# Layer 2 of an attention and two-MLP kernel, in blocks of 512 tokens

## The chip, the core and the metric

The kernel runs on one core of a Trainium2 chip. TensorE (PE) multiplies matrices: it loads a weight tile and streams columns past it into a bank of PSUM. VectorE (DVE), ScalarE (ACT) and GpSimd (POOL) do elementwise work, SyncE (SP) issues the DMAs. The metric is device time of one execution in microseconds (us), the median of several runs. The granted clock is the share of TensorE's full speed of 2.4 GHz that the chip allows; its other level is 1.2 GHz.

## The reference

Three stages, one after the other. The first is a linear-attention recurrence over 768 steps, for 4 batches and 8 heads of width 40. Its output, 3072 tokens of 320 values, goes through two layers of one form:

```python
x = attn_out.transpose(0, 2, 1, 3).reshape(3072, 320)
h = np.maximum(x @ w_in, 0.0)      # layer 1: w_in 320 x 2048
x = h * h @ w_out                  # w_out 2048 x 320
h = x @ w_in2                      # layer 2, weights of its own
r = np.maximum(h, 0.0)
out = (r * r) @ w_out2
```

## The kernel before

**Recording and planning.** The kernel does not issue its instructions as it meets them. Each call is recorded as a task with the cells of memory that it reads and writes. `_Plan.run` (L320) then plays the tasks through a model of the five engines: it has a cost for each form, and for each engine a heap of ready tasks ordered by `plan.prio`, lowest first. Whichever engine is free earliest takes its best ready task. The order that comes out is fixed; on the chip each engine runs its own list in that order and waits for semaphores. `plan.either` (L181) records a task that can go to one of several engines; for DVE the planner asks whether another engine would be done within 800 model ns of it, and if so leaves the task there. All recorded instructions have the line L69, so tiles and shapes tell them apart.

**Split numbers.** Every product is made of numbers split in a high and a low part (`xh`, `xl` and so on), and of the four partial products three are computed, so a matrix product is three matmuls.

**The two layers.** 3072 tokens are 12 blocks of 256 (`NBLK`). The hidden width of 2048 is 16 slices f of 128 (`NF`). `in_step` (L899) makes one slice: eight matmuls of 256 columns, weights `wi` stationary, tokens moving, into one bank (`HB`, banks 4 and 5). `gate` (L1001) makes relu, square, the high part `m_h` and the low part `m_l` of the slice, three of them in flight (`NG`). Relu and square are ACT's; the cast to `m_h` may go to ACT or DVE, the subtraction for `m_l` to DVE or POOL. `out_step2` (L938) of layer 2 then makes, for both halves of 128 tokens, three matmuls of 320 columns with the gate stationary and `wo` moving; two banks gather the 16 slices. Even and odd blocks use banks 0, 1 and 2, 3. `block2` (L1095) runs this for a block, copies the two banks to `m_o`, one on ACT and one on DVE, and sends them out in four DMAs. Layer 1 (`block1`, L1008) has its output transposed: 16 matmuls of 256 columns per slice, gathered in banks 6 and 7, and a zeroing matmul of 512 columns at the start of each block.

**The order of stages.** Attention, the decoding of layer 1's weights and layer 1 are planned together until the attention is over (L1078). Then layer 2's weights get their room and are decoded (`decode_w2`, 36 pieces of a DMA and some ten elementwise instructions on ACT, DVE and POOL); what is left of layer 1 and all of layer 2 is recorded and run. Gates have priorities from -200 up, inputs -100 (`P_X`), decoding 2.7 (`P_D`), matmuls from 1000 up (L1023). So PE does the earliest block first and takes a later slice when an earlier gate is not ready. `load_x` (L948) puts a block's input in the one staging tile `m_x`; `split_x` (L953) splits it into `m_xh` and `m_xl`, two buffers for even and odd blocks, used by both layers. `check_w` (L1126) tests the decays' range with 16 reductions on DVE.

Of the kernel before, what the change touches and what calls it, by code (L numbers as in the profile page):

```python
# [26 lines left out]
NF = 16  # L27
# [45 lines left out]
class _Plan:  # L73
# [5 lines left out]
    def __init__(self, nc):  # L79
        self.V = _Engine(self, nc.vector, "DVE")  # L80
        self.A = _Engine(self, nc.scalar, "ACT")
        self.G = _Engine(self, nc.gpsimd, "POOL")
        self.T = _Engine(self, nc.tensor, "PE")
        self.D = _Engine(self, nc.sync, "SP")
        self.tasks = []
        self.wr, self.rd = {}, {}
        self.cache = {}
        self.prio = 0.0
        self.tag = None
        self.open = None  # L90
        self.left = {}
        self.done = {}
        self.free = dict.fromkeys(self.LAT, 0.0)
        self.avail = {e: [] for e in self.LAT}
        self.pend = {e: [] for e in self.LAT}
        self.succ = {}
        self.npred = {}
        self.ready = {}
        self.mode = None
        self.first = None  # L100
        self.ticks = {}
        self.dma = 0.0
        self.held = {}

    def group(self):
        return _Group(self)
# [71 lines left out]
        else:  # L178
            self.add([rec])

    def either(self, *calls):  # L181

        alts, first = {}, None
        for f in calls:
            self.open = []
            f()
            recs, self.open = self.open, None
            first = first or recs
            alts[recs[0][0]] = ([r[1] for r in recs], sum(r[2] for r in recs), max(r[5] for r in recs))
        self.add(first, alts)  # L190

    def add(self, ops, alts=None):
        if not ops:
            return
        i = len(self.tasks)
# [31 lines left out]
        alts = alts or {eng: ([o[1] for o in ops], cost, max(o[5] for o in ops))}  # L227
        self.tasks.append((alts, self.prio, nbytes, self.tag, k))
        self.left[self.tag] = self.left.get(self.tag, 0) + 1
        live = [q for q in preds if q not in self.done]  # L230
        self.npred[i] = len(live)
        self.ready[i] = dict.fromkeys(alts, 0.0)
# [3 lines left out]
            else:  # L236
                self.succ.setdefault(q, []).append(i)
        if not live:
            for e in alts:
                heapq.heappush(self.pend[e], (self.ready[i][e], i))  # L240

    def after(self, q, i):
        t, e = self.done[q]
# [76 lines left out]
    def run(self, until=None):  # L320
        while until is None or self.left.get(until, 0):
# [57 lines left out]
            for j in self.succ.pop(i, ()):  # L379
                self.after(i, j)  # L380
                self.npred[j] -= 1
                if not self.npred[j]:
                    for z in self.tasks[j][0]:
                        heapq.heappush(self.pend[z], (self.ready[j][z], j))


@with_exitstack
def rwkv7_two_mlp_kernel(
# [60 lines left out]
    dx = [mm[:, 2304:3264], mm[:, 3264:4224]]  # L449
    nid0 = moe.tile([128, 192], F32R, name="nid")  # L450
    nid = nid0[:, 64:192]
    m_xh = [moe.tile([128, 3, 256], F32R, name=f"m_xh{i}") for i in range(2)]
    m_xl = [moe.tile([128, 3, 256], F32R, name=f"m_xl{i}") for i in range(2)]
    m_h = [moe.tile([128, 256], F32R, name=f"m_h{i}") for i in range(NG)]
    m_l = [moe.tile([128, 256], F32R, name=f"m_l{i}") for i in range(NG)]
    m_x = pad[:, 0:768].rearrange("p (k t) -> p k t", k=3)
# [305 lines left out]
    def copy(engs, o, i):  # L762
        calls = []
        for eng in engs:
            calls.append((lambda: A.copy(out=o, in_=i)) if eng is A else (lambda eng=eng: eng.tensor_copy(out=o, in_=i)))
        plan.either(*calls)
# [14 lines left out]
    def add(eng, o, x, y):  # L781
        tt2(eng, o, x, y, ALU.add)
# [155 lines left out]
    def out_step2(w, f, i, ob):  # L938
        gh = m_h[i % NG]
        gl = m_l[i % NG]  # L940
        for s in range(2):
            o = slice(s * 128, s * 128 + 128)
            with plan.group():
                T.matmul(ob[s][:, 0:320], gh[:, o], w[2][:, f, 0:320], start=(f == 0), stop=False)
                T.matmul(ob[s][:, 0:320], gh[:, o], w[2][:, f, 320:640], start=False, stop=False)
                T.matmul(ob[s][:, 0:320], gl[:, o], w[2][:, f, 0:320], start=False, stop=(f == NF - 1))

    def load_x(src_a, src_b):  # L948
        D.dma_start(out=m_x[:, 0:2], in_=src_a)
        for s in range(2):  # L950
            D.dma_start(out=m_x[64 * s:64 * s + 64, 2], in_=src_b)

    def split_x(xh, xl):  # L953
        copy(AV, xh, m_x)
        sub(VG, xl, m_x, xh.bitcast(F32))
# [43 lines left out]
        V.memset(bank[i], 0.0)  # L999

    def gate(h, i):  # L1001
        gg, gh, gl = m_r[i % 2], m_h[i % NG], m_l[i % NG]
        A.activation(out=gg, in_=h, func=AF.Relu)
        A.activation(out=gg, in_=gg, func=AF.Square)
        copy(AV, gh, gg)
        sub(VG, gl, gg, gh.bitcast(F32))

# [74 lines left out]
    def make_w2():  # L1082
        pool = w2x.enter_context(tc.tile_pool(name="w2", bufs=1))
        w = alloc_w(pool, 2)
        d = [pool.tile([128, 960], F32, name=f"dt{i}") for i in range(2)]
        plan.prio = P_D
        decode_w2(w, win2, win32, wout2, dx + d)
        return w, d, pool
# [6 lines left out]
    def block2(m, at, rows):  # L1095
# [14 lines left out]
        for s in range(2):  # L1110
# [3 lines left out]
            for h in range(2):  # L1114
                D.dma_start(out=rows(s, h), in_=o[64 * h:64 * h + 64])

    orow = out.rearrange("(p s u t) d -> p s u t d", p=NP, s=2, u=NU)
    wflat = nat[3].rearrange("b t d -> (b t d)").rearrange("(p x) -> p x", p=128)
    WC = wflat.shape[1]
# [20 lines left out]
        V.tensor_reduce(out=wrow[:, 256:257], in_=wrow[:, 0:256], axis=AX.X, op=ALU.max)  # L1140
        V.tensor_copy(out=wbad, in_=wrow[:, 256:257])

    for m in range(NBLK):
        block2(m, m, lambda p, s: orow[p, s, m])
        if m == min(3, NBLK - 1):
            check_w()
    plan.run()
    sched.__exit__(None, None, None)
# [45 lines left out]
    with tc.If(bad > 0):  # L1194
        with tc.tile_pool(name="gen", bufs=1) as gen:
            general_attention(gen)
        w2 = make_w2()[0]
        plan.run()
        with tc.For_i(0, NU) as q:
            block1(0, q)  # L1200
            block2(0, q, lambda p, s: orow[p, s, bass.ds(q, 1)].rearrange("o t d -> (o t) d"))
            plan.run()
        w2x.close()
# [78 lines left out]
```

## Time and profile before

| | us |
|---|---|
| median of 3 runs | 1207.71 (1205.3 to 1211.73) |
| profiled execution | 1209.43 |
| its span, first to last instruction | 1207.6 |
| PE busy | 1104.0 (91%) |
| DVE, ACT, POOL busy | 805.9, 747.5, 388.2 |
| mean granted clock | 0.955 |

A busy time is an average over stages. Until about 716 us the attention and layer 1 share the engines; then layer 1 and the decoding of layer 2's weights; from about 876 us layer 2 is alone. An instruction of the profile stands as output tile <- input tiles; PE's duration of one matmul is longer than the distance between two, since they overlap, so the distance of starts is what counts.

### The profile page before, as it was taken

The numbers are of one execution on the slowest core, as the hardware profiler recorded it, in microseconds if no ns is written. First come the engines' busy times: TensorE is split into PE (matmuls) and PEld (weight loads), VectorE is DVE, ScalarE is ACT, GpSimd is POOL, SyncE is SP. The second block draws the span as 40 slices with busy tenths as digits, with TensorE's granted clock in tenths as the row PEclk, the third lists the DMA queues.
The fourth block names the chain that finished last, engine by engine and source line by source line (L and its number), as shares of the span: only waits on it lengthen the run. The fifth ranks groups of instructions, "written<-read, shape, count | busy, mean of one in ns | idle before, by whom it ended". The sixth has DMA issues, their size and how long they took to land.

```text
span 1207.6 us, 43193 instructions
## 1 busy us (share of the span) xinstructions
PE 1104.0 (91%) x18096; PEld 1032.2 (85%) x18096; DVE 805.9 (67%) x1786; ACT 747.5 (62%) x2077; POOL 388.2 (32%) x443
## 2 busy tenths in 40 slices
PE   3888898998989998899899999999899999999996
PEld 2656787887878887798789899999899999999996
DVE  6887888789888978999798746666773232222221
ACT  4496554555565565556446468888666666666664
POOL 7544334223323332343224117776820000000000
PEclk9986789999998999999899999999899999999999
DMA  8555343155325515533451322332241010101000
GB/s 244 143 154 146 85 104 103 57 127 146 79 70 138 136 49 127 143 90 78 123 121 36 60 74 84 93 93 82 79 140 36 25 29 24 33 24 27 13 12 14
DMA packets 142239, 103.86 MB, mean 86 GB/s; under 512 B 98001, under 2 KB 110162, under 8 KB 142034
## 3 DMA queue, kind: packets, MB, share of 16 engines
q1 hardware_dynamic: 142034, 101.00, 31.5%
q8 instruction: 144, 2.36, 0.8%
q14 instruction: 61, 0.50, 0.1%
HBM read 82.88 MB, written 11.80 MB: 78 GB/s over the span
## 4 chain that ended last, share of the span: by engine, by line
PE 50%; DVE 7%; ACT 3%; issue 2%; DMA 1%; POOL 1%; SPq 1%; DVEq 0%; ACTq 0%; POOLq 0%
PE bank L69 50%; DVE mm L69 3%; DVE q L69 2%; ACT mm L69 1%; ACT q L69 1%; SPq L69 1%; DVE x L69 0%; DVE y L69 0%; DVE kt L69 0%; ACT m_h L69 0%; DMA v<-in_el_dram 0%; POOL kb L69 0%; DMA lk<-kt 0%; DVE p L69 0%; DMA mm<-in_win_dram 0%
## 5 line engine op out<-in xcount | busy, mean ns | idle before, releaser
L69 PE MATMUL bank<-m_xh,wi 128*128 128x256 f32 x1920 | 387.0, 286 | 9.7 <-ACT mm L69 5.4
L69 POOL TENSOR_TENSOR m_l<-mm,m_h 128x256 fp32r<-128x256 f32 x200 | 162.8, 816 | 546.3 <-ACT m_h L69 293.7
L69 PEld LDWEIGHTS bank<-m_xh,wi 128*128 128x128 f32 x1920 | 315.3, 193 | 13.2 <-ACT mm L69 6.0
L69 PE MATMUL bank<-m_xl,wi 128*128 128x256 f32 x1152 | 324.2, 285 | 1.8 <-POOL m_xl L69 1.8
L69 ACT ACTIVATE mm<-bank 128x256 f32<-128x256 f32 x384 | 146.2, 382 | 233.1 <-PE bank L69 214.3
L69 DVE TENSOR_TENSOR m_l<-mm,m_h 128x256 fp32r<-128x256 f32 x184 | 85.0, 462 | 217.6 <-ACT m_h L69 209.7
L69 PEld LDWEIGHTS bank<-m_xl,wi 128*128 128x128 f32 x1152 | 222.3, 193 | 2.3 <-POOL m_xl L69 2.3
L69 ACT ACTIVATE mm<-mm 128x256 f32<-128x256 f32 (+3 forms) x500 | 205.0, 423 | 30.6 <-POOL m_xl L69 14.8
L69 PE MATMUL bank<-m_h,wo 128*128 128x256 f32 x960 | 206.7, 297 | 0.1
L69 PE MATMUL bank<-wo,m_h 128*128 128x320 f32 x768 | 172.5, 311 | 1.7 <-ACT m_h L69 1.2
L69 PEld LDWEIGHTS bank<-m_h,wo 128*128 128x128 f32 x960 | 156.6, 192 | 10.0 <-issue 1.4
L69 PE MATMUL bank<-m_l,wo 128*128 128x256 f32 x576 | 156.6, 284 | 0.1
L69 ACT CAST m_h<-mm 128x256 fp32r<-128x256 f32 x359 | 145.1, 405 | 10.2 <-PE bank L69 1.9
L69 PEld LDWEIGHTS bank<-wo,m_h 128*128 128x128 f32 x768 | 125.7, 190 | 2.2 <-ACT m_h L69 1.4
L69 PE MATMUL bank<-wo,m_l 128*128 128x320 f32 x384 | 119.2, 310 | 1.0 <-POOL m_l L69 1.0
L69 DVE TENSOR_TENSOR mm<-mm 128x30 f32<-128x30 f32 (+9 forms) x317 | 106.0, 334 | 8.4 <-ACT wi L69 0.7
L69 PEld LDWEIGHTS bank<-m_l,wo 128*128 128x128 f32 x576 | 110.7, 192 | 0.5 <-POOL m_l L69 0.3
L69 DVE TENSOR_TENSOR q<-bank,cs 32x128 f32<-32x128 f32 (+1 forms) x240 | 87.7, 366 | 30.6 <-ACT q L69 22.2
L69 PE MATMUL bank<-q,lk 128*40 128x72 f32 x1536 | 63.7, 233 | 23.7 <-DVE q L69 10.6
L69 PEld LDWEIGHTS bank<-q,lk 128*40 128x40 f32 x1536 | 53.7, 120 | 31.7 <-ACT mm L69 9.9
L69 ACT COPY q<-bank 40x256 f32<-40x256 f32 (+1 forms) x168 | 54.6, 325 | 37.3 <-PE bank L69 33.6
L69 ACT ACTIVATE q<-bank 32x160 f32<-32x160 f32 x192 | 56.6, 295 | 27.3 <-PE bank L69 24.8
(135 smaller groups left out, 1633.1 us busy)
## 6 DMA issues: line engine op xcount, KB each, us to landing
kb<-in_el_dram SPq DMA_DIRECT2D x24, 512.0 KB
mm<-in_win_dram SPq DMA_DIRECT2D x30, 256.0 KB
a<-in_el_dram SPq DMA_DIRECT2D x24, 256.0 KB
v<-in_el_dram SPq DMA_DIRECT2D x24, 256.0 KB
r<-in_er_dram SPq DMA_DIRECT2D x24, 256.0 KB
lk<-kt SPq DMA_DIRECT2D x96, 64.0 KB
mm<-in_wr_dram SPq DMA_DIRECT2D x20, 260.0 KB
mm<-in_wout_dram SPq DMA_DIRECT2D x20, 256.0 KB
```

The source lines that it names most:

```text
L69: self.plan.op(self, op, lambda: getattr(self.real, op)(*args, **kw), outs, ins, kw)
```

## The change

Layer 2 works on six wide blocks of two old blocks each (`wide2`). `in_wide` makes a slice for 512 tokens with eight matmuls of 512 columns; it has four banks for slices (4 to 7). `out_wide` makes four times three matmuls of 320 columns, into banks 0 to 3, which all blocks share. The buffers of the wide gates lie where layer 1's weights were (`gw`, the tile `wo1`), those of odd blocks' inputs too (`xw`, the tile `wi1`); even blocks use both old input buffers. At a block's end four banks go through the two tiles `m_o`. Relu and square become tasks for ACT or DVE; with `late=True` they are offered to ACT alone as long as tasks of the attention are left. `check_w` comes after the second wide block, as it came after the fourth block. The last part of the diff belongs to a branch that runs only where the decays are out of range.

```diff
+    def push(self, i):
+        only = i in self.late and self.left.get("att", 0)
+        for e in list(self.tasks[i][0])[:1 if only else None]:
+            heapq.heappush(self.pend[e], (self.ready[i][e], i))
...
-    m_xh = [moe.tile([128, 3, 256], F32R, name=f"m_xh{i}") for i in range(2)]
-    m_xl = [moe.tile([128, 3, 256], F32R, name=f"m_xl{i}") for i in range(2)]
+    x_h, x_l = (moe.tile([128, 2, 3, 256], F32R, name=z) for z in ("m_xh", "m_xl"))
+    m_xh, m_xl = ([z[:, i] for i in range(2)] for z in (x_h, x_l))
...
+    def in_wide(xh, xl, f, h):
+        o = slice(f * 128, (f + 1) * 128)
+        seq = []
+        for i in range(2):
+            seq += [(w2[0][:, 0, i, o], xh[:, :, i]), (w2[0][:, 0, i, o], xl[:, :, i]), (w2[0][:, 1, i, o], xh[:, :, i])]
+        seq += [(w2[1][:, o], xh[:, :, 2]), (w2[1][:, o], xl[:, :, 2])]
+        h = h.rearrange("p (b t) -> p b t", b=2)
+        for q in range(2):
+            with plan.group():
+                for i, (z, x) in enumerate(seq[4 * q:4 * q + 4]):
+                    T.matmul(h, z, x, start=(q + i == 0), stop=(q == 1 and i == 3))
+
+    def out_wide(f, gh, gl, ob):
+        for s in range(4):
+            o = slice(s * 128, s * 128 + 128)
+            with plan.group():
+                T.matmul(ob[s], gh[:, o], w2[2][:, f, 0:320], start=(f == 0), stop=False)
+                T.matmul(ob[s], gh[:, o], w2[2][:, f, 320:640], start=False, stop=False)
+                T.matmul(ob[s], gl[:, o], w2[2][:, f, 0:320], start=False, stop=(f == NF - 1))
...
     def gate(h, i):
-        gg, gh, gl = m_r[i % 2], m_h[i % NG], m_l[i % NG]
-        A.activation(out=gg, in_=h, func=AF.Relu)
-        A.activation(out=gg, in_=gg, func=AF.Square)
+        gate_to(h, m_r[i % 2], m_h[i % NG], m_l[i % NG])
+
+    def gate_to(h, gg, gh, gl):
+        plan.either(
+            lambda: A.activation(out=gg, in_=h, func=AF.Relu),
+            lambda: V.tensor_scalar(out=gg, in0=h, scalar1=0.0, scalar2=None, op0=ALU.max),
+            late=True,
+        )
+        plan.either(
+            lambda: A.activation(out=gg, in_=gg, func=AF.Square),
+            lambda: V.tensor_tensor(out=gg, in0=h, in1=gg, op=ALU.mult),
+            late=True,
+        )
         copy(AV, gh, gg)
         sub(VG, gl, gg, gh.bitcast(F32))
...
+    xw = w1[0].rearrange("p i s f -> p (i s f)")
+    gw = w1[2].rearrange("p f d -> p (f d)")
+    xs = [(x_h, x_l), tuple(xw[:, o:o + 1536].rearrange("p (b k t) -> p b k t", b=2, k=3) for o in (0, 1536))]
+    ghs, gls = ([gw[:, o + 512 * i:o + 512 * i + 512] for i in range(NG)] for o in (0, 512 * NG))
+    ggs = [mm[:, 1792:2304], cs[:, C_D1:C_D1 + 512]]
+
+    def wide2(m):
+
+        xh, xl = xs[m % 2]
+        ob = [bank[i][:, 0:320] for i in range(4)]
+        for b in range(2):
+            plan.prio = P_X + m
+            load_x(x2a[2 * m + b].rearrange("p (k t) -> p k t", k=2), x2b[2 * m + b])
+            split_x(xh[:, b], xl[:, b])
+        for f in range(NF):
+            i = m * NF + f
+            j = NBLK * NF + i
+            h = bank[4 + i % 4]
+            plan.prio = P_M + j
+            in_wide(xh, xl, f, h)
+            plan.prio = P_G + j
+            gate_to(h, ggs[i % 2], ghs[i % NG], gls[i % NG])
+            plan.prio = P_M + j + 1.5
+            out_wide(f, ghs[i % NG], gls[i % NG], ob)
+        plan.prio = P_G + j
+        for s in range(4):
+            o = m_o[s % 2]
+            copy(((A, V)[s % 2],), o, ob[s])
+            for k in range(2):
+                D.dma_start(out=orow[s % 2, k, 2 * m + s // 2], in_=o[64 * k:64 * k + 64])
...
-    for m in range(NBLK):
-        block2(m, m, lambda p, s: orow[p, s, m])
-        if m == min(3, NBLK - 1):
+    for m in range(NBLK // 2):
+        wide2(m)
+        if m == min(1, NBLK // 2 - 1):
             check_w()
```

The planner makes a new order from the end of the attention on; before it the two lists are the same. PE, a step of layer 2 in the middle of the stage, in the kernel before: one slice into bank 4 (`wi2`, `wi3_2` are layer 2's first weights), then the outputs of an earlier one (`wo2`) into banks 0 and 1.

```order
L69 MATMUL bank4_71<-m_xh0_83,wi2_11703 128x256
L69 MATMUL bank4_71<-m_xl0_85,wi2_11703 128x256
L69 MATMUL bank4_71<-m_xh0_83,wi2_11703 128x256 x2
L69 MATMUL bank4_71<-m_xl0_85,wi2_11703 128x256
L69 MATMUL bank4_71<-m_xh0_83,wi2_11703 128x256
L69 MATMUL bank4_71<-m_xh0_83,wi3_2_11704 128x256
L69 MATMUL bank4_71<-m_xl0_85,wi3_2_11704 128x256
L69 MATMUL bank0_67<-wo2_11705,m_h0_87 128x320 x2
L69 MATMUL bank0_67<-wo2_11705,m_l0_90 128x320
L69 MATMUL bank1_68<-wo2_11705,m_h0_87 128x320 x2
L69 MATMUL bank1_68<-wo2_11705,m_l0_90 128x320
```

In the changed kernel, for 512 tokens of an odd block (tokens in `wi1`, gates in `wo1`):

```order
L69 MATMUL bank4_71<-wi1_123,wi2_11701 128x512 x6
L69 MATMUL bank4_71<-wi1_123,wi3_2_11702 128x512 x2
L69 MATMUL bank0_67<-wo2_11703,wo1_125 128x320 x3
L69 MATMUL bank1_68<-wo2_11703,wo1_125 128x320 x3
L69 MATMUL bank2_69<-wo2_11703,wo1_125 128x320 x3
L69 MATMUL bank3_70<-wo2_11703,wo1_125 128x320 x3
```

Eight matmuls of 512 columns stand where two times eight of 256 stood; the twelve of 320 columns are as many for 512 tokens as before.

PE where layer 2 begins, in the kernel before: the last two matmuls of layer 1's last `in_step` (`wi3_1`), one output step of layer 1 (`wo1`), and the first of layer 2, on input buffer 0 of each pair.

```order
L69 MATMUL bank5_72<-m_xh1_84,wi3_1_126 128x256
L69 MATMUL bank5_72<-m_xl1_86,wi3_1_126 128x256
L69 MATMUL bank6_73<-m_h0_87,wo1_127 128x256 x2
L69 MATMUL bank6_73<-m_l0_90,wo1_127 128x256
L69 MATMUL bank6_73<-m_h0_87,wo1_127 128x256 x2
L69 MATMUL bank6_73<-m_l0_90,wo1_127 128x256
L69 MATMUL bank7_74<-m_h0_87,wo1_127 128x256
L69 MATMUL bank7_74<-m_l0_90,wo1_127 128x256
L69 MATMUL bank4_71<-m_xh0_83,wi2_11703 128x256
L69 MATMUL bank4_71<-m_xl0_85,wi2_11703 128x256
L69 MATMUL bank4_71<-m_xh0_83,wi2_11703 128x256 x2
```

The same place in the changed kernel; the input tiles `m_xh` and `m_xl` now hold both halves.

```order
L69 MATMUL bank5_72<-m_xh_83,wi3_1_124 128x256
L69 MATMUL bank5_72<-m_xl_84,wi3_1_124 128x256
L69 MATMUL bank6_73<-m_h0_85,wo1_125 128x256 x2
L69 MATMUL bank6_73<-m_l0_88,wo1_125 128x256
L69 MATMUL bank6_73<-m_h0_85,wo1_125 128x256 x2
L69 MATMUL bank6_73<-m_l0_88,wo1_125 128x256
L69 MATMUL bank7_74<-m_h0_85,wo1_125 128x256
L69 MATMUL bank7_74<-m_l0_88,wo1_125 128x256
L69 MATMUL bank4_71<-m_xh_83,wi2_11701 128x512
L69 MATMUL bank4_71<-m_xl_84,wi2_11701 128x512
L69 MATMUL bank4_71<-m_xh_83,wi2_11701 128x512 x2
```

The first wide matmuls stand at the same place, behind the same output step, but read both input buffers, also the one that the layer-1 matmuls just above read.

DVE in the steady part of layer 2, in the kernel before: low parts of gates, an input (768 columns), a bank to copy out.

```order
L69 TENSOR_TENSOR m_l2_92<-mm_81,m_h2_89 128x256
L69 TENSOR_TENSOR m_l0_90<-mm_81,m_h0_87 128x256
L69 CAST m_xh0_83<-mm_81 128x768
L69 TENSOR_TENSOR m_xl0_85<-mm_81,m_xh0_83 128x768
L69 TENSOR_TENSOR m_l0_90<-mm_81,m_h0_87 128x256
L69 COPY mm_81<-bank1_68 128x320
L69 TENSOR_TENSOR m_l1_91<-mm_81,m_h1_88 128x256
```

In the changed kernel: two gates in a row (relu, square, cast, subtraction, from banks 6 and 7).

```order
L69 TENSOR_SCALAR mm_81<-bank6_73 128x512
L69 TENSOR_TENSOR mm_81<-bank6_73,mm_81 128x512
L69 CAST wo1_125<-mm_81 128x512
L69 TENSOR_TENSOR wo1_125<-mm_81,wo1_125 128x512
L69 TENSOR_SCALAR cs_66<-bank7_74 128x512
L69 TENSOR_TENSOR cs_66<-bank7_74,cs_66 128x512
L69 CAST wo1_125<-cs_66 128x512
L69 TENSOR_TENSOR wo1_125<-cs_66,wo1_125 128x512
```

DVE has whole gates of 512 columns here, where it had the last step of gates of 256. Of the 96 wide gates DVE has the relu of 68 and the square of 63.

## Rows read from the trace of the kernel before

**Rows 1.** Stretches of the span; columns are named in the first row.

```profile
core 0: us, PE busy (x) PEld busy (x) DVE busy (x) ACT busy (x) POOL busy (x), PEclk, DMA share, GB/s
716.00:834.00 118.00, 117.91 (x1005) 117.52 (x1006) 71.16 (x130) 98.05 (x281) 82.81 (x97) 1.00 0.31 92
839.00:858.80 19.80, 19.80 (x152) 19.80 (x152) 11.90 (x23) 16.47 (x47) 13.90 (x18) 1.00 0.29 85
858.80:875.60 16.80, 12.74 (x61) 11.33 (x60) 13.57 (x20) 10.79 (x30) 14.39 (x16) 0.70 0.28 82
875.60:1198.50 322.90, 322.88 (x2454) 322.59 (x2452) 103.97 (x209) 208.90 (x532) 20.59 (x24) 1.00 0.13 34
```

**Rows 2.** Chain of waits, in order of time: start us, us, what.

```profile
855.62 2.69 DMA mm<-in_win_dram
...
868.71 329.78 PE bank L69 x2487
```

**Rows 3.** Timeline of PE in layer 2: start us, us, instruction.

```profile
1002.37 0.28 PE L69 MATMUL bank<-m_xh,wi 128*128 128x256 f32 x1
1002.49 0.28 PE L69 MATMUL bank<-m_xl,wi 128*128 128x256 f32 x1
...
1003.33 0.46 PE L69 MATMUL bank<-wo,m_h 128*128 128x320 f32 x2
...
1004.21 0.28 PE L69 MATMUL bank<-m_xh,wi 128*128 128x256 f32 x1
```

**Rows 4.** Timeline of PE, a zeroing matmul of layer 1.

```profile
809.45 0.39 PE L69 MATMUL bank<-nid 128*128 128x512 f32 x1
809.68 0.40 PE L69 MATMUL bank<-m_h,wo 128*128 128x256 f32 x2
```

**Rows 5.** Timeline of PE in and behind the stretch of low clock.

```profile
858.83 0.46 PE L69 MATMUL bank<-wo,m_h 128*128 128x320 f32 x2
...
871.44 0.41 PE L69 MATMUL bank<-m_xl,wi 128*128 128x256 f32 x1
871.65 0.63 PE L69 MATMUL bank<-m_xh,wi 128*128 128x256 f32 x2
...
875.57 0.46 PE L69 MATMUL bank<-wo,m_h 128*128 128x320 f32 x2
```

**Rows 6.** Timeline of PE where layer 2 begins.

```profile
832.08 0.40 PE L69 MATMUL bank<-m_h,wo 128*128 128x256 f32 x2
...
836.61 0.38 PE L69 MATMUL bank<-m_xh,wi 128*128 128x256 f32 x1 [0.58 <-ACT mm L69]
```

**Rows 7.** Groups by shape, ACT, 700 to 1200 us; columns as on the page.

```profile
L69 ACT CAST m_xh<-mm 128x768 fp32r<-128x768 f32 x10 | 8.3, 831 | 2.5 <-PE bank L69 2.5
```

**Rows 8.** Groups by shape, DVE, 700 to 1200 us.

```profile
L69 DVE TENSOR_TENSOR m_l<-mm,m_h 128x256 fp32r<-128x256 f32 x168 | 75.3, 448 | 204.7 <-ACT m_h L69 201.5 <-PE bank L69 1.9 <-POOL m_l L69 0.9
L69 DVE TENSOR_TENSOR m_xl<-mm,m_xh 128x768 fp32r<-128x768 f32 x12 | 11.5, 958 | 6.1 <-ACT m_xh L69 5.6
...
L69 DVE TENSOR_TENSOR wo<-dt 128x320 fp32r<-128x320 f32 x8 | 6.4, 804 | 8.6 <-POOL dt L69 8.6
...
L69 DVE CAST m_h<-mm 128x256 fp32r<-128x256 f32 x14 | 4.1, 290 | 5.1 <-ACT mm L69 5.0
...
L69 DVE TENSOR_TENSOR mm<-mm 128x320 f32<-128x320 f32 x3 | 1.4, 481 | 0.0
```

**Rows 9.** Groups by shape, DVE, whole span.

```profile
L69 DVE TENSOR_TENSOR x<-bank,cs 32x512 f32<-32x512 f32 x38 | 26.0, 683 | 2.2 <-PE bank L69 1.2
```

**Rows 10.** Timeline of ACT, DVE and SP at the end.

```profile
1198.08 0.43 ACT L69 COPY mm<-bank 128x320 f32<-128x320 f32 x1 [0.96 <-PE bank L69]
...
1198.52 0.49 DVE L69 COPY mm<-bank 128x320 f32<-128x320 f32 x1 [0.94 <-PE bank L69]
1198.54 3.25 SPq L69 DMA_DIRECT2D out_dram<-mm  x4
```

More of the change, by code (lines that the diff above doesn't have):

```diff
@@ L103, in __init__ @@
         self.held = {}
+        self.late = set()
     def group(self):
@@ L179, in op, with either @@
             self.add([rec])
-    def either(self, *calls):
+    def either(self, *calls, late=False):
         alts, first = {}, None
@@ L189, in either, with add @@
             alts[recs[0][0]] = ([r[1] for r in recs], sum(r[2] for r in recs), max(r[5] for r in recs))
-        self.add(first, alts)
-    def add(self, ops, alts=None):
+        self.add(first, alts, late)
+    def push(self, i):
+        only = i in self.late and self.left.get("att", 0)
+        for e in list(self.tasks[i][0])[:1 if only else None]:
+            heapq.heappush(self.pend[e], (self.ready[i][e], i))
+    def add(self, ops, alts=None, late=False):
         if not ops:
@@ L229, in add @@
         self.left[self.tag] = self.left.get(self.tag, 0) + 1
+        if late:
+            self.late.add(i)
         live = [q for q in preds if q not in self.done]
@@ L238, in add @@
         if not live:
-            for e in alts:
-                heapq.heappush(self.pend[e], (self.ready[i][e], i))
+            self.push(i)
     def after(self, q, i):
@@ L382, in run @@
                 if not self.npred[j]:
-                    for z in self.tasks[j][0]:
-                        heapq.heappush(self.pend[z], (self.ready[j][z], j))
+                    self.push(j)
 @with_exitstack
@@ L1196, in rwkv7_two_mlp_kernel @@
             general_attention(gen)
+        D.dma_start(out=cs[:, 0:C_D1], in_=cst[:, 0:C_D1])
+        plan.prio = P_D
+        decode_w1(w1, win1, win31, wout1)
         w2 = make_w2()[0]
```

## The prediction, made before the changed kernel ran

> **What bounds the kernel now.** I read the profile in four steps: the busy times of chosen stretches, to find where TensorE (PE) is the bound; the chain of waits, to see what the end hangs on; the timeline of PE, for the price of one matmul of each width; and the groups of instructions by shape, for the engines that feed PE. The reader should see this. From 716 us, when the attention is over, PE is busy in 117.91 of 118.00 us, and from 875.6 to 1198.5 us in 322.88 of 322.90, at clock 1.00 [rows 1]. The chain says the same: its last long piece is 329.78 us of PE, 2487 matmuls in a row that wait for nobody [rows 2]. ScalarE (ACT) and VectorE (DVE) are busy for 208.90 and 103.97 us of the 322.9, so the other engines are not the bound of layer 2. There is one hole: from 858.8 to 875.6 us PE is busy 12.74 of 16.80 us and its granted clock is 0.70 [rows 1]. A layer-2 change can therefore gain in two ways only: fewer PE nanoseconds for the same columns, and the hole.
>
> **The price of a matmul.** In the steady stretch eight 256-column matmuls take 1002.37 to 1003.33 us, 120 ns each, and the six 320-column ones that follow take until 1004.21 us, 147 ns each [rows 3]. 64 more columns cost 27 ns, which is 2.4 columns a nanosecond; so each matmul carries the same 13 ns on top of its columns, whatever its width. For 512 columns that gives 213 + 13 = 226 ns. The trace has this width once per layer-1 block: the zeroing matmul on bank 6 starts at 809.45 us and the next matmul at 809.68 us, 230 ns by these rounded rows [rows 4]. I take 227.
>
> The Trainium skill ("TensorE: Matmul & The Clock Gate", section "Back-to-back issue gap") says a warm matmul costs its columns plus only 6 cycles: 262 cycles for 256, 518 for 512. By that rule two calls merged into one would save 2.5 ns. The trace does not agree: 120 ns for 256 columns is 288 cycles of 2.4 GHz. By the page the first term below would be 1.9 us in place of 10.0.
>
> **The change part by part.**
>
> *Width.* Per pair of 256-token blocks and per slice f of the hidden layer, sixteen 256-column matmuls become eight of 512. Six wide blocks by 16 slices by 8 are 768 merged pairs, each 2 x 120 - 227 = 13 ns: **-10.0 us**. The second matmul of a slice keeps its 12 calls of 320 columns for 512 tokens, so nothing is won there. A slice now lasts 8 x 0.227 + 12 x 0.147 = 3.58 us, where two slices of 1.84 us stood. Ends: 0 (a 512 call costs two of 256) and -15 us (it carries no more than half of the 13 ns).
>
> *The hole.* It is layer 2 overtaking the decoding of its own weights. PE starts 58 matmuls between 858.83 and 875.57 us [rows 5]. At full pace they are 18 x 0.147 + 40 x 0.120 = 7.45 us; they took 16.74, so **9.3 us** are lost, some 4 us waiting for gates and decoded weights, the rest because the granted clock fell to its lower level after those waits (871.44 to 871.65 us, 0.21 for one 256-column matmul, where 0.12 is usual) [rows 5]. Layer 2 begins at about 833 us and is at slice 11 or so when it stalls. In the changed kernel a slice takes 3.58 us, so slice 14 is wanted near 833 + 14 x 3.58 = 883 us, while in the old trace PE waits for decoded weights for the last time at 868.71 us [rows 2]. In the changed order the last decode instruction on DVE stands ahead of the gate of slice 7. So this loss should go: **-9.3 us**; ends: -9.3, and 0 if something else opens a hole of this size.
>
> *The wider input.* The first wide block needs the inputs of two old blocks. One lies in the buffer that layer 1's last block reads; it can be rewritten only after that block's last `in_step`, which ends at about 832.1 us [rows 6]. Then come ACT's cast (0.83 us [rows 7]) and DVE's subtraction (0.96 us [rows 8]) of 768 columns, about 2.1 us with hand-overs, and PE has only eight matmuls (8 x 0.12 = 0.96 us) to do meanwhile: +1.2 us. Its third and fourth slices use banks 6 and 7, which must first be copied out for layer 1: +0.5. The old entry had a wait of its own of 0.58 us [rows 6], which goes. Sum **+1.1**; ends 0 and +8 (the wait is long enough to bring the lower clock, as in the hole).
>
> *The gates.* A gate of 512 columns on DVE is: relu 0.69 and square 0.69 (0.683 for 512 columns out of PSUM [rows 9]), cast about 0.58 (twice 0.290), subtraction 0.70 (half way between 0.448 for 256 and 0.958 for 768 [rows 8]): 2.7 us. The DVE order below has most gates of the steady stretch whole on DVE: 2.7 of 3.58 us, one after the other. PE wants the result only after the next slice's eight wide matmuls and the preceding slice's twelve narrow ones, again 3.58 us. So it is hidden with about 0.9 us to spare: **0**. If DVE ran at the pace it has next to a busy GpSimd (0.804 against 0.481 for 320 columns [rows 8]) the four would take 4.5 us and the cover would be gone; GpSimd is busy 20.59 of 322.90 us there [rows 1], so I do not expect it. In layer 1 between 716 and 833 us PE is full already, so moving gates from ACT to DVE has nothing to win: 0, at most 1 us either way.
>
> *Block ends.* Four banks are copied out through two staging buffers, so the third copy waits until the first one's DMA has read its buffer. DVE also splits the next input there. Old layer 2 has no idle PE at its block ends [rows 1]. PE now has one or two slices to go on with; I charge 0.3 us for each of 5 ends: **+1.5**; ends 0 and +10 (2 us each, about one DMA of 2.69 us [rows 2] uncovered).
>
> *The tail.* The last gate (2.7 us plus hand-over) has only one slice of narrow matmuls (1.76 us) in front of it: +0.9. After the last matmul the old kernel copies its second bank (0.49 us) and issues four DMAs in 3.25 us, 0.81 each [rows 10]; with 2.69 us for a DMA [rows 2] the last one lands 0.05 + 3 x 0.81 + 2.69 = 5.2 us behind the last matmul. Now the first copy ends 0.9 us before it and its second DMA lands at -0.9 + 0.8 + 2.7 = 2.6; the second copy's DMAs follow on the same queue and land at 4.2, the fourth copy ends at 4.7 and its second DMA lands at 4.7 + 0.8 + 2.7 = 8.2. That is +3.0; the DMAs are smaller than the one priced here, so I take +2.5. **+3.4** in all; ends +1 and +5.
>
> Sum: -10.0 - 9.3 + 1.1 + 1.5 + 3.4 = **-13.3 us**. The profiled execution took 1209.43 us (span 1207.6, 1.8 around it), so it would take 1196.1; it stood 1.7 above the median of the three runs (1207.71), so I forecast a median of **1194 us**.
>
> **Rivals.**
>
> 1. *The wider matmul saves nothing* (240 ns for 512). For: the only 512-column row streams a broadcast zero, not real data in two pieces. Against: 256 and 320 columns carry the same 13 ns. Time 1194 + 10 = 1204, within 0.5%. Chance 0.10. The page named above comes out near it, at 1202.
> 2. *The hole moves.* The wait at the entry of layer 2, with banks 6 and 7 late too, lasts long enough for the lower clock, and some 8 us of the 9.3 are given back: 1202. For: 1.7 us of waits stand there on one spot. Against: behind the wait of 0.58 us at 836 us [rows 6] the clock stayed at 1.00 [rows 1]. Chance 0.12.
> 3. *Slower: DVE becomes the bound.* Place: the steady stretch; price: what four DVE instructions exceed 3.58 us by, for some 65 of 96 slices. At 4.5 us that is 0.9 x 65 = 60 us, so about 1254; it decides from about 3.8 us on, where the 13 us gained are used up (13 / 65 = 0.2). For: DVE takes nearly all gates in the new order while ACT is left free. Against: the sum of 2.7 us. Chance 0.06.
> 4. *More is won*: the 512 call carries less overhead and the block ends cost nothing, 1187. Chance 0.08.
> That the DVE does not take gates at all is excluded by the order.
>
> **How the numbers follow.** The forecast has 0.64, with a range of its own of 1189 to 1199. Within 0.5% means 1201.7 to 1213.7, about what a measurement of this kernel can tell from no change. Faster: 0.64 + 0.08 + about a third of rivals 1 and 2 = 0.79; same: the rest of these two = 0.14; slower 0.07. A range of 1186 to 1204 holds cases 1, 2, 4 and the forecast but for their edges.
>
> **What would show it.** Wide matmuls starting 227 ns apart, and slices 3.58 us apart; no stretch of clock below 1.00 between 835 and 1180 us; last matmul near 1182 us with some 11 us behind it; a wait of 1 to 2 us of PE for the first wide input. Wrong would be: 240 ns per wide matmul, a lower clock at the entry, or PE waiting for DVE's gates at every slice.

## The result, and the profile after

The changed kernel took 1189.6 us (median of 4 runs, 1186.75 to 1199.25) beside 1207.23 us of the kernel before (4 runs, 1205.3 to 1211.73): ratio 0.9889, 95% interval 0.9845 to 0.9932 (the ratio on record; the quotient of these two medians is 0.985). The forecast was 1194. The profiled execution took 1186.75 us, its span 1184.9, against 1209.43 and 1207.6.

These 22.7 us must be cut in two. Up to the attention's end PE's instructions have the same order in both kernels. Behind the last attention matmul stands the zeroing matmul of layer 1; here it is in the changed kernel's PE timeline (start us, us, instruction):

```profile
704.37 1.20 PE L69 MATMUL bank<-q,lk 128*40 128x72 f32 x32
705.50 0.51 PE L69 MATMUL bank<-nid 128*128 128x512 f32 x1
```

and in that of the kernel before:

```profile
715.88 0.51 PE L69 MATMUL bank<-nid 128*128 128x512 f32 x1
```

So 10.4 of the 22.7 us arose before anything that the change moves. From the start of the last attention matmul to the end it is 491.9 us before and 479.5 after: **-12.4 us**. That is the number to hold against the predicted sum of -13.3.

Stretches of the changed kernel, columns as in [rows 1]:

```profile
716.00:834.00 118.00, 117.43 (x966) 115.36 (x965) 77.22 (x128) 100.95 (x284) 88.54 (x101) 1.00 0.32 93
834.00:860.00 26.00, 26.00 (x152) 23.99 (x151) 15.75 (x26) 18.48 (x38) 19.60 (x19) 1.00 0.29 83
860.00:900.00 40.00, 40.00 (x224) 36.24 (x223) 28.39 (x34) 23.04 (x42) 19.54 (x17) 1.00 0.49 138
900.00:1170.00 270.00, 270.00 (x1496) 243.74 (x1496) 177.94 (x288) 23.59 (x41) 6.67 (x5) 1.00 0.07 18
1170.00:1185.00 15.00, 2.61 (x15) 1.82 (x13) 2.11 (x5) 0.85 (x2) 0.00 (x0) 0.71 0.22 49
```

The stretch with a clock of 0.70 and PE busy 12.74 of 16.80 us in [rows 1] has no counterpart: PE is full at clock 1.00 from 834 to 1170 us. DVE now works 177.94 of 270 us, ACT 23.59: the gates have changed engines, and neither is near the bound. The chain of waits (start us, us, what) says the same; where [rows 2] had PE alone only from 868.71 us, its last piece now begins with layer 2:

```profile
822.50 0.97 DVE m_xl L69
823.51 345.05 PE bank L69 x1911
1173.99 2.97 DMA out_dram<-mm
```

The steady stretch in PE's timeline, against [rows 3]:

```profile
1002.98 2.02 PE L69 MATMUL bank<-wi,wi 128*128 128x512 f32 x8
1004.84 2.80 PE L69 MATMUL bank<-wo,wo 128*128 128x320 f32 x18
1007.48 2.02 PE L69 MATMUL bank<-wi,wi 128*128 128x512 f32 x8
```

Eight wide matmuls take 1.86 us, 232 ns each (not 227); 18 narrow ones take 2.64 us, 147 ns each as before. Of DVE's groups from 900 to 1170 us (columns as in [rows 8]) these four make one set of gates:

```profile
L69 DVE TENSOR_SCALAR cs<-bank 128x512 f32<-128x512 f32 x32 | 22.1, 692 | 35.4 <-PE bank L69 35.4
L69 DVE TENSOR_TENSOR cs<-bank,cs 128x512 f32<-128x512 f32 x32 | 22.1, 692 | 1.1
L69 DVE CAST wo<-cs 128x512 fp32r<-128x512 f32 x33 | 14.1, 427 | 3.3 <-ACT cs L69 2.3
L69 DVE TENSOR_TENSOR wo<-cs,wo 128x512 fp32r<-128x512 f32 x35 | 24.3, 693 | 5.1 <-ACT wo L69 4.0
```

0.692 + 0.692 + 0.427 + 0.693 = 2.50 us per gate (2.7 was predicted), and the idle time stands in front of the first of them, ended by PE: DVE waits for PE at each slice, not PE for DVE. At the entry of layer 2, against [rows 6]:

```profile
822.16 0.28 PE L69 MATMUL bank<-m_l,wo 128*128 128x256 f32 x1
822.52 0.50 PE L69 MATMUL bank<-m_xh,wi 128*128 128x512 f32 x1
823.51 0.50 PE L69 MATMUL bank<-m_xl,wi 128*128 128x512 f32 x1 [0.49 <-DVE m_xl L69]
823.85 0.63 PE L69 MATMUL bank<-m_xh,wi 128*128 128x512 f32 x2
```

PE waits for the subtraction of the second half of the first input, 1.1 us over its usual pace, and the clock holds. At the end, ACT, DVE and SP, against [rows 10]:

```profile
1171.75 0.43 ACT L69 COPY mm<-bank 128x320 f32<-128x320 f32 x1 [53.40 <-PE bank L69]
1176.67 0.43 ACT L69 COPY mm<-bank 128x320 f32<-128x320 f32 x1 [4.50 <-DMA out_dram<-mm]
...
1172.14 0.49 DVE L69 COPY mm<-bank 128x320 f32<-128x320 f32 x1 [0.95 <-PE bank L69]
1177.09 0.49 DVE L69 COPY mm<-bank 128x320 f32<-128x320 f32 x1 [4.45 <-PEq L1262]
...
1172.20 8.05 SPq L69 DMA_DIRECT2D out_dram<-mm  x8
```

The third copy waits 4.50 us for the first one's DMA. From the start of the last matmul to the end it is 12.2 us, where 9.5 stood.

### The profile page after: what moved, and what is told of

The parts are those of the page before. It is cut to its first block, busy times and chain, and to the rows that moved or that the text cites. A ratio compares the mean times of both kernels' runs of the same rounds, so it can differ in the third digit from the quotient of the medians.

```text
span 1184.9 us, 40953 instructions
## 1 busy us (share of the span) xinstructions
PE 1083.9 (91%) x17328; PEld 979.1 (83%) x17328; DVE 910.7 (77%) x1891; ACT 580.5 (49%) x1599; POOL 396.2 (33%) x432
## 4 chain that ended last, share of the span: by engine, by line
PE 51%; DVE 8%; ACT 3%; issue 2%; DMA 1%; POOL 0%; SPq 0%; DVEq 0%; ACTq 0%; POOLq 0%
PE bank L69 51%; DVE mm L69 3%; DVE q L69 2%; ACT q L69 1%; ACT mm L69 1%; DVE x L69 1%; DVE y L69 0%; DVE kt L69 0%; ACT m_h L69 0%; SPq L69 0%; DMA v<-in_el_dram 0%; DMA out_dram<-mm 0%; DMA lk<-kt 0%; DVE w L69 0%; DVE p L69 0%
## 5 line engine op out<-in xcount | busy, mean ns | idle before, releaser
L69 PE MATMUL bank<-m_xh,wi 128*128 128x256 f32 (+1 forms) x1200 | 271.2, 307 | 2.9 <-ACT m_xh L69 1.3
L69 PE MATMUL bank<-m_xl,wi 128*128 128x256 f32 (+1 forms) x720 | 218.3, 306 | 2.6 <-POOL m_xl L69 2.1
L69 PEld LDWEIGHTS bank<-m_xh,wi 128*128 128x128 f32 x1200 | 201.2, 191 | 13.9 <-ACT m_xh L69 1.8
L69 PE MATMUL bank<-wo,wo 128*128 128x320 f32 x1152 | 184.6, 309 | 0.4 <-DVE wo L69 0.4
L69 PEld LDWEIGHTS bank<-wo,wo 128*128 128x128 f32 x1152 | 176.7, 188 | 9.2 <-DVE wo L69 0.9
L69 ACT ACTIVATE mm<-mm 128x256 f32<-128x256 f32 (+4 forms) x323 | 135.9, 438 | 37.4 <-POOL m_xl L69 15.4
L69 ACT ACTIVATE mm<-bank 128x256 f32<-128x256 f32 (+1 forms) x202 | 79.6, 396 | 138.7 <-PE bank L69 121.9
L69 PEld LDWEIGHTS bank<-m_xl,wi 128*128 128x128 f32 x720 | 137.6, 191 | 7.2 <-POOL m_xl L69 2.5
L69 DVE TENSOR_TENSOR mm<-mm 128x30 f32<-128x30 f32 (+8 forms) x316 | 104.6, 331 | 8.3 <-ACT wi L69 0.7
L69 PE MATMUL bank<-wi,wi 128*128 128x512 f32 x384 | 97.4, 395 | 0.0
L69 PE MATMUL bank<-q,lk 128*40 128x72 f32 x1536 | 62.5, 231 | 21.7 <-DVE q L69 11.7
```

What stands on the lines that cost most here:

```text
L69: self.plan.op(self, op, lambda: getattr(self.real, op)(*args, **kw), outs, ins, kw)
```

## The experiments

The table has the part from the last attention matmul to the end, one profile each, and the medians with that of the kernel before in the same set of runs.

| kernel | attention's end to end, us | median, us (runs) | before beside it | ratio, 95% |
|---|---|---|---|---|
| before | 491.9 | | | |
| changed | 479.5 | 1189.6 (4) | 1207.23 | 0.9889, 0.9845 to 0.9932 |
| e4_again (changed) | 479.3 | 1190.58 (4) | 1201.11 | 0.9896, 0.9841 to 0.9952 |
| e13_after_beside (changed) | 478.8 | 1190.05 (6) | 1201.3 | 0.9908, 0.9873 to 0.9944 |
| e1_split | 483.8 | 1194.94 (10) | 1201.11 | 0.9929, 0.99 to 0.9959 |
| e2_act_gates | 479.8 | 1189.8 (6) | 1203.02 | 0.9891, 0.983 to 0.9951 |
| e3_late_only | 492.2 | 1204.98 (10) | 1201.11 | 1.0027, 0.9993 to 1.0061 |
| e5_decode_first | 509.7 | 1221.05 (4) | 1201.11 | 1.0145, 1.0066 to 1.0225 |
| e10_decode_sooner | 489.7 | 1199.15 (10) | 1203.02 | 0.9965, 0.9937 to 0.9992 |
| e8_flat_x | 487.1 | 1194.59 (10) | 1203.02 | 0.9935, 0.9905 to 0.9964 |
| e12_flat_odd | 478.9 | 1191.58 (1) | 1201.3 | |
| e6_four_out | 478.2 | 1186.73 (4) | 1203.02 | 0.9872, 0.981 to 0.9934 |
| e11_best | 475.5 | 1186.9 (6) | 1201.3 | 0.9868, 0.9833 to 0.9903 |

**The width alone: e1_split.**

```diff
-        for q in range(2):
+        for b in range(2):
             with plan.group():
-                for i, (z, x) in enumerate(seq[4 * q:4 * q + 4]):
-                    T.matmul(h, z, x, start=(q + i == 0), stop=(q == 1 and i == 3))
+                for i, (z, x) in enumerate(seq):
+                    T.matmul(h[:, b], z, x[:, b], start=(i == 0), stop=(i == 7))
```

> The changed kernel with each 512-column matmul of layer 2 issued as two 256-column ones; the wide blocks, the gates and the schedule stay. In the profiles the part from the last attention matmul to the end took 491.9 us before and 479.5 after. Theory A: the hole of 9.3 us went because a wide block asks for its weights later and gates come in one piece, and the width itself is worth 768 x (2 x 120 - 232) = 6 us. Then this part takes 479.5 + 6 = 486, no granted clock under 1.00 stands between 835 and 1170 us, and a slice takes 3.68 us. Theory B (the prediction's price of 227 ns, so a gain of 10 us by the width): 489 to 490. Rival C: the hole went because fewer instructions are queued on PE in front of each gate; then it comes back here, with a stretch of lower clock within 30 us of layer 2's start, and the part takes 490 to 496.

Measured 483.8, 4.3 to 5.0 us over the three profiles of the changed kernel, and no hole. PE's timeline:

```profile
1002.18 1.92 PE L69 MATMUL bank<-wo,wo 128*128 128x320 f32 x12
1003.93 2.05 PE L69 MATMUL bank<-wi,wi 128*128 128x256 f32 x16
1005.82 1.92 PE L69 MATMUL bank<-wo,wo 128*128 128x320 f32 x12
```

and a stretch, columns as in [rows 1]:

```profile
835.00:1170.00 335.00, 335.00 (x2560) 335.00 (x2559) 215.75 (x333) 70.77 (x130) 59.49 (x49) 1.00 0.15 40
```

Sixteen matmuls of 256 columns take 1.89 us here, 118 ns each, where they took 120 before. This is an odd block, whose input lies in layer 1's weight tile: behind 860 us such matmuls of e1 took 118.5 ns in the mean (768 of them), those on the old input buffers 119.8, as in the kernel before. The mean over the slices behind 860 us is 1.906 us against 1.856 of the changed kernel: the width is worth 0.050 x 96 = 4.8 us, 4 to 5 with the totals. Theory A holds with a smaller size; B (10 us) and C (the hole comes back) fall. So it is not the wider matmul that closes the hole, but something else in the wide block.

**The gates alone, on narrow blocks: e3_late_only**, and **the wide blocks without them: e2_act_gates.** The first has the kernel before with

```diff
-        A.activation(out=gg, in_=h, func=AF.Relu)
-        A.activation(out=gg, in_=gg, func=AF.Square)
+        plan.either(
+            lambda: A.activation(out=gg, in_=h, func=AF.Relu),
+            lambda: V.tensor_scalar(out=gg, in0=h, scalar1=0.0, scalar2=None, op0=ALU.max),
+            late=True,
+        )
...
```

and the second the changed kernel with the opposite edit.

> The kernel before, with narrow 256-token blocks in layer 2, and only the second part of the change: relu and square of a gate may go to DVE once the attention has ended. Theory A (the hole is layer 2 overtaking the decoding of its weights, and only the wide block slows the demand): the hole stays, within 4 us of its 9.3, and the part from the attention's end to the end takes 488 to 494 us (491.9 before). Rival D: gates on DVE are what closed the hole; then the part takes 482 to 484 and no clock under 1.00 stands behind 835 us. Rival E: DVE, which also decodes, is delayed by the gates, the hole grows: over 496.

> The changed kernel with relu and square of every gate on ACT, as before; the wide blocks stay. A 512-column gate on ACT is some 0.6 + 0.6 us by twice the halves' rows, with cast and subtraction 2.5 to 2.9 us of the 3.61 of a slice, so either engine has room. Theory A (the gates' engine has no part in the gain): the part from the attention's end to the end takes 479.5 us within 2, and no clock under 1.00 stands from 835 to 1170 us. Rival D (DVE's gates closed the hole): the hole comes back, 485 to 492. Rival H (ACT now delays banks or decoding): a hole or waits in the last 40 slices of layer 1, over 483.

e3 took 492.2 and kept its hole, as theory A has it:

```profile
852.00:874.00 22.00, 17.71 (x97) 16.11 (x96) 19.29 (x29) 13.01 (x36) 17.37 (x19) 0.77 0.36 103
```

e2 took 479.8, PE full all through layer 2, with ACT busy 187.10 us and DVE 111.76:

```profile
825.00:1165.00 340.00, 340.00 (x1884) 307.11 (x1883) 111.76 (x159) 187.10 (x325) 50.17 (x42) 1.00 0.14 40
```

So the second half of the change gains nothing on either kind of block; D, E and H fall.

**The decoding earlier, on narrow blocks: e5_decode_first and e10_decode_sooner.**

```diff
-        plan.prio = P_D
+        plan.prio = P_D - 300.0
```

and with 12.0 in e10. In the code the gate of slice j, counted through both layers, has priority -200 + j. The old 2.7 therefore stands behind all of layer 1's gates and those of layer 2's first eleven slices; -9.3 stands behind layer 1's gates but the last, and ahead of all of layer 2's. The seventeen slices of layer 1 in e10's expectation are a miscount; e5's -297.3 is ahead of every gate.

> The kernel before with one number changed: the decoding of layer 2's weights is put 300 ahead in the order of priority, so DVE, ACT and POOL decode ahead of the gates of layer 1 where both are ready. Theory A (the hole is a lag of the decoding): the hole vanishes or shrinks to under 3 us, and the part from the attention's end to the end falls from 491.9 to 483 to 486 us unless layer 1's gates now come late. Rival F (the hole is a lag of gates on ACT, not of weights): the hole stays at 9 us or grows, 492 or more. Either way the steady slices stay at 8 x 120 + 6 x 147 = 1.84 us.

> The kernel before with one number changed: the decoding of layer 2's weights goes 12 slices ahead in priority, so ahead of the gates of the last 17 slices of layer 1, not of all that are left (300 ahead took the hole out of layer 2, whose part from the first output matmul to the last fell from 358.6 to 351.3 us, but the last 40 slices of layer 1 lost 26). Theory A (the hole is the decoding's lag, and moving it buys the hole with waits of layer 1): the hole is gone or halved (first output matmul to last 351 to 355) and layer 1 loses 0 to 15, so 484 to 499 from the attention's end, where 491.9 stood before. Rival L (the decode could have been moved for free, so the wide block wasn't needed for this part of the gain): 484 or less.

In e5 the hole of layer 2 is gone, but layer 1 pays for it:

```profile
713.00:861.00 148.00, 131.62 (x1038) 127.03 (x1033) 118.32 (x169) 117.86 (x320) 118.11 (x134) 0.95 0.35 107
861.00:1213.00 352.00, 352.00 (x2680) 351.97 (x2678) 104.68 (x223) 228.73 (x583) 17.69 (x20) 1.00 0.10 28
```

From the first output matmul of layer 2 to the last it took 351.3 us (358.6 before), but layer 1 ended 25.6 us later after the attention. What PE waits for in that first stretch (what; us in total, times, longest us) is mostly low parts of gates, and once, at the end of a block of layer 1, the taking of its result out of a bank. Both engines named, POOL and DVE, are busy there for 118 of 148 us, with decoding ahead of them in the order:

```profile
PE bank L69 <- POOL m_l L69: 10.2, 9, 3.1
PE bank L69 <- DVE mm L69: 3.6, 1, 3.6
```

Its total of 509.7 missed the 483 to 486 that I gave for the undisturbed case, and by the total alone rival F (492 or more) would fit; it is the place of the loss, layer 1 and not the hole, that speaks against F. In e10 the trade is mild: layer 1 loses 1.9 us, layer 2 gains 4.1 and never sees the lower clock, though PE still waits:

```profile
831.00:870.00 39.00, 35.40 (x261) 33.89 (x260) 32.94 (x47) 31.68 (x88) 31.15 (x36) 1.00 0.37 110
870.00:1186.00 316.00, 316.00 (x2405) 315.98 (x2403) 97.35 (x199) 205.72 (x523) 19.20 (x22) 1.00 0.12 30
```

Its waits from 716 to 1175 us, all ended by gates (the third and last kind, for `m_l` on DVE, is 0.2 us):

```profile
PE bank L69 <- ACT mm L69: 2.9, 4, 1.5
PE bank L69 <- POOL m_l L69: 1.7, 2, 1.4
```

Theory A holds; F and L fall. Decoding and gates share DVE, ACT and POOL, and with narrow blocks these two orders mostly chose who waits: the better of them gained 2.2 us in all. The wide block does something else: it asks later.

**The layout of the input: e8_flat_x, then e12_flat_odd.**

```diff
-    xs = [(x_h, x_l), tuple(xw[:, o:o + 1536].rearrange("p (b k t) -> p b k t", b=2, k=3) for o in (0, 1536))]
+    xs = [tuple(z.rearrange("p b k t -> p (b k t)").rearrange("p (k b t) -> p b k t", b=2, k=3) for z in (x_h, x_l)), tuple(xw[:, o:o + 1536].rearrange("p (k b t) -> p b k t", b=2, k=3) for o in (0, 1536))]
```

e12 keeps `(x_h, x_l)` for the even blocks and has the new form, `(k b t)`, for the odd ones.

> The changed kernel with the input of a wide block laid out so that the 512 moving columns of a matmul lie in one piece, where they were two pieces of 256. A 512-column call was 227 ns by my prediction and takes 231 (even blocks) or 233 ns (odd ones). Theory J (the two pieces cost the 4 to 6 ns): 227 ns or less, 768 x 5 = 3.8 us less, 475.6 from the attention's end. Theory K (it is the matmul itself, and the place of its result): 229 to 233 again, and 479.4 within 1 us.

> The changed kernel with the input laid out in one piece of 512 columns in the odd wide blocks alone; the even ones, the first among them, keep two pieces. With the one-piece layout in all blocks the part from the attention's end took 487.1 us and not 479.4, with 8 us of waits and low clock where layer 2 begins, while its steady slices were the same. Theory O (there the first block's two halves interleave in both old input buffers, so its casts start only when layer 1 has read both; that is the whole loss): 479.4 within 1 here, no clock under 1.00 near 820 to 845 us. Rival P (the one-piece layout costs something per block, by splitting into strided pieces): 483 or more.

Eight wide matmuls took 1.856 us in the mean in both, as in the changed kernel: theory K, the two pieces cost nothing. But e8 took 487.1. PE where layer 2 begins:

```profile
825.26 0.39 PE L69 MATMUL bank<-m_l,wo 128*128 128x256 f32 x1 [1.26 <-POOL m_l L69]
...
826.88 0.28 PE L69 MATMUL bank<-m_l,wo 128*128 128x256 f32 x1
829.02 0.50 PE L69 MATMUL bank<-m_xh,wi 128*128 128x512 f32 x1 [1.86 <-ACT m_xh L69]
830.97 0.79 PE L69 MATMUL bank<-m_xl,wi 128*128 128x512 f32 x1 [1.44 <-POOL m_xl L69]
...
832.41 0.63 PE L69 MATMUL bank<-m_xl,wi 128*128 128x512 f32 x1
832.84 1.05 PE L69 MATMUL bank<-m_xh,wi 128*128 128x512 f32 x2
```

and the stretch around it (columns as in [rows 1]):

```profile
826.00:842.00 16.00, 12.70 (x50) 10.18 (x50) 11.96 (x18) 11.20 (x24) 11.93 (x11) 0.79 0.47 141
```

A wait of 1.26 us for a gate of layer 1, then two of 1.86 and 1.44 us for the input, and with them the lower clock: 0.43 us between wide matmuls (832.41 to 832.84). This is my second rival, the hole moved to the entry, at just the price that I gave it (8 us), in a kernel that differs from the changed one by a layout. e12 took 478.9 with clock 1.00 there, so theory O, as far as it says that the even blocks' layout is the loss. That the casts come late because the halves interleave in both old buffers, and because the second must wait for the one staging tile, is read from the code and was not tried apart.

**The tail: e6_four_out and e11_best.**

```diff
-            o = m_o[s % 2]
+            o = m_o[s % 2] if s < 2 else mm[:, 2304 + 320 * (s - 2):2624 + 320 * (s - 2)]
```

and in e11 also

```diff
-                D.dma_start(out=orow[s % 2, k, 2 * m + s // 2], in_=o[64 * k:64 * k + 64])
+                (D, A)[k if m == NBLK // 2 - 1 else 0].dma_start(out=orow[s % 2, k, 2 * m + s // 2], in_=o[64 * k:64 * k + 64])
```

> The changed kernel with four staging buffers for a wide block's output instead of two, so no copy waits for an output DMA. From the start of the last matmul to the end it took 12.2 us in the changed kernel (11.9 in its second profile) and 9.5 before. Theory A (the third and fourth copies wait for the first two's DMAs): 9.2 to 9.9, so 479.4 becomes 477; the block ends, which cost nothing already, stay. Rival I (the tail is the eight DMA issues of 0.8 us each one after the other on SP, whichever buffers they read): 11 to 12, no gain.

> The changed kernel with four staging buffers for the output (which took the tail from 11.9 to 12.2 us to 10.9) and, for the last wide block alone, every second output DMA issued by ACT in place of SP. Theory M (the rest of the tail is SP's eight issues in a row, 6.8 us of 10.9): with four issues on each of two queues the last issue ends some 3.4 us earlier, so 7.2 to 8 from the last matmul's start to the end, and 475 from the attention's end. Rival N (the landing of the DMAs is the bound, or ACT's issues hold its own copies back): over 9.5.

e6: the copies no longer wait, but the tail is 10.9 us, 0.6 to 1.3 less, between what theory A and rival I gave. SP's queue shows the rest:

```profile
1172.50 6.80 SPq L69 DMA_DIRECT2D out_dram<-mm  x8
```

Eight issues of 0.85 us in a row follow the first copy. In e11 four of them stand on ACT:

```profile
1177.44 3.63 SPq L69 DMA_DIRECT2D out_dram<-mm  x4
...
1177.45 0.56 ACTq L69 DMA_DIRECT2D out_dram<-mm  x1
...
1178.20 2.88 ACTq L69 DMA_DIRECT2D out_dram<-mm  x3
```

The tail is 8.2 us (7.2 to 8 expected, so a little over), 475.5 in all: theory M. The Trainium skill ("DMA: Bandwidth & Descriptors", section "Issuing engines are not separate DMA queues") says that starting DMAs from several engines saves only the time of issuing, usually small beside the DMA; here that time was the larger part of the tail, and 3.3 us less than in the changed kernel's run beside it is what both edits together gave. The medians, 1186.9 and 1190.05, agree in size, but their intervals overlap.

**The changed kernel again: e4_again and e13_after_beside.**

> The changed kernel as it is, a second time. The two profiles differ by 22.7 us, of which 10.4 lie before the attention's end, where the order of instructions is the same in both. Theory A: this 10.4 is the granted clock of that execution and not the change; then the part up to the attention's end comes out anywhere between 703 and 718 us here, and the part behind it at 479.5 within 1 us. Rival G: the change does something to the first part (placement of buffers, loading of code); then 705 comes again within 1 us, and the other kernels of this set with the narrow blocks show 715 again.

> The changed kernel as it is, beside the version with the shorter tail on the same chip: 479.4 us from the attention's end within 1, and 3 to 5 us slower in the median than the version with the shorter tail. The part up to the attention's end, the same order of instructions in all, varies by some 10 us between executions.

The last attention matmul stands at 704.6 us in e4 and at 710.7 in e13 (705.3 at first); the narrow e10 has 706.3, e3 712.1 and the kernel before 715.7. e2 even 701.1. So this part varies by some 10 us and more whichever kernel runs, and rival G falls by e13 and e10. That the granted clock makes the difference, as theory A adds, is not shown: its mean over this part was 0.96 in e2 and 0.95 in e4, but 0.94 with 705.3, 710.7 and 715.7 us alike. The part behind it repeats within 0.7 us. The changed kernel's gain in the median is 10.5 and 11.3 us in these two sets and 17.6 in the first.

## Why the prediction was right, and where it was not

The forecast held, with the median near the lower end of its own range of 1189 to 1199; the hole's mechanism was right, and the width was mis-sized.

| step | predicted, us | measured, us |
|---|---|---|
| width | -10.0 | -6.3 |
| hole | -9.3 | -9.3 |
| entry | +1.1 | +0.3 |
| gates on DVE | 0 | 0 |
| block ends | +1.5 | 0 |
| tail | +3.4 | +3.6 |
| sum | -13.3 | -11.7 by parts, -12.4 as a whole |

*Width.* The term was mis-sized. A pair of narrow slices took 3.680 us in the mean, a wide slice takes 3.614: 0.066 x 96 = 6.3 us. e1 shows 4 to 5 of them to be the width. The rest came with the wide block without the width: 118.5 ns in place of 119.7 for 256 columns where the input lies in layer 1's weight tile, and 146.6 in place of 147.0 for 320. Longer runs of one kind are not the reason for the first: in the kernel before, runs of sixteen took 119.8 ns a matmul, those of eight 119.6. I had carried the 13 ns on top of 256 and 320 columns to 512; measured, 512 columns carry 232 - 213 = 19 ns. The nearest row, the zeroing matmul at 230 ns [rows 4], was the better guide, and I rounded it down. By the rule of the Trainium skill that the prediction weighed ("TensorE: Matmul & The Clock Gate", section "Back-to-back issue gap"), which the page gives for an isolated matmul and not for a stream, a merged pair would save 2.5 ns; the trace does not agree: 2 x 119 - 232 = 6 ns by e1's mean and 2 x 120 - 232 = 8 ns against the kernel before lie between it and my 13.

*The hole.* Right in size, and in cause as far as the runs can tell. In the kernel before, PE's waits in the hole are these (850 to 880 us; us in total, times, longest):

```profile
PE bank L69 <- ACT m_h L69: 1.2, 1, 1.2
PE bank L69 <- POOL m_l L69: 1.0, 1, 1.0
PE bank L69 <- DVE wi L69: 0.8, 1, 0.8
PE bank L69 <- DVE wo L69: 0.6, 1, 0.6
PE bank L69 <- POOL wi L69: 0.5, 1, 0.5
```

Of 4.1 us gates ended 2.2 and weights 1.9. That the weights are the limit is seen when the 16 slices of `wo` and their first uses are counted off in the traces: the outputs of slices 12 to 15 start within 1 us of the end of their slice's decoding in the kernel before, 8.5 us or more behind it in the changed kernel, and 5.3 or more in e1. Sooner gates would have met undecoded weights. That it is demand and not supply shows in when decoding ends. In the changed kernel its last instruction on POOL is

```profile
874.99 1.22 POOL L69 TENSOR_TENSOR wo<-dt 128x320 fp32r<-128x320 f32 x1
```

that is 170.9 us after the last attention matmul; in the kernel before the last was on DVE,

```profile
875.62 1.03 DVE L69 TENSOR_TENSOR wo<-dt 128x320 fp32r<-128x320 f32 x1
```

161 us after it. Decoding even ends 10 us later, and nobody waits for it, since a wide block uses each slice of the weights for 3.6 us and not for 1.8. e1 has the same without the wide matmul; e3 and e2 exclude the gates' change of engine. The wide block also has four banks for slices in place of two, and gives a gate a longer cover; no run takes these apart from the later demand, so how much of the gates' 2.2 us they would have removed alone is open. One reading of mine was wrong without harm: on DVE the last decoding instruction (869.64 us) stands behind the gate of slice 11 (867.07), not ahead of that of slice 7.

*Entry.* 1.1 us are lost there, close to the 1.2 that I gave the input; banks 6 and 7, charged with 0.5, held nobody up, and the old kernel lost 0.8 at the same place, not only the 0.58 that I took off. e8 shows that the bound of +8 was real.

*Block ends.* No group of matmuls at a block's end is off its pace: the copies' wait for DMAs lies beside a slice or two of PE's work. The charge was caution without a row.

*The tail.* Right in sum: 0.9 us before the last matmuls (the last gate) and 2.7 behind. My two absolute tails, 5.2 and 8.2 us, were both some 4 us short of the 9.5 and 12.2 measured from the start of the last matmul; that this cancels in the difference is luck. The reason was half of it. I named the two staging buffers; e6 shows that they were 0.6 to 1.3 us, and e11 that the row of issues on SP was as much and more.

*The median.* 1194 against 1189.6: the kernel before shrinks by 12.4 us, and the rest of the first set's 17.6 is the spread of the part up to the attention's end, which the sum cannot know. The errors of width (+3.7) and of block ends and entry (-2.3) partly cancelled, which is luck too: the forecast is better than its terms.

0.7 us of the 12.4 are in none of these steps; 0.4 of them lie in layer 1, where 980 matmuls in place of 977 started in the first 115 us behind the attention. Open too is why 512 columns carry 19 ns: it is not the two pieces (e8, e12).

## What to carry to other kernels

When a consumer catches up with the decoding of its own weights, working on more rows per weight slice can close the gap without making the decoding faster; moving the decoding forward here mostly moved the wait. Price a wider instruction by the nearest row of that very width, not by a line through narrower ones. At a kernel's end count the DMA issues on one queue before blaming buffers.

## What the runs showed of the hardware

- In layer 2 one matmul's pace at granted clock 1.00 was 118 to 120 ns for 256 columns, 147 for 320, and 232 for 512: on top of 2.4 columns a nanosecond 11 to 13, 13 and 19 ns. By the place of the moving tile the 512-column one took 230.8 (old input buffers, 300 matmuls behind 860 us) and 232.7 (layer 1's weight tile, 384).
- In e8 the lower clock came with waits of PE of 1.26, 1.86 and 1.44 us that ended at 825.26, 829.02 and 830.97 us. In e10 the two longest waits, 1.5 and 1.4 us, ended at 834.66 and 857.48 us, PE was idle 3.6 of the 39 us around them, and the clock stayed at 1.00; so did it in the changed kernel behind its one wait of 0.49 us at the entry.
- DVE's cast of 512 columns took 0.427 us, not twice the 0.290 of 256 [rows 8].
